# A recurrent attention, a mixture of experts and a feed-forward pair in one kernel: another way out of PSUM for the outputs, another order for the copies of the decays, whole third transposes, and a new price for strided copies

## The chip, the cores and the metric

The kernel runs on one core of a Trainium2 chip. The metric is the device time of one execution in microseconds, lower is better. The core has TensorE (PE, matrix products; PEld is its weight load), VectorE (DVE), ScalarE (ACT), GpSimd (POOL) and SyncE (SP, which here issues DMAs). Each engine works through its own queue in order.

## The reference

Three stages follow one another, all in float32.

```
# 1: 4 batches x 8 heads = 32 states of 40x40, 768 steps
y[t]  = r[t] . state
Sa    = state . a[t]
state = state * w[t] - outer(Sa, b[t]) + outer(v[t], k[t])
# 2: x = y as 3072 tokens x 320; 8 experts, the best one for each token
h = relu(x_e @ w1[e]);  out = gate * (h @ w2[e])        # 320 -> 1024 -> 320
# 3: h = out @ w_in;  g = max(h,0) + alpha*min(h,0);  result = g @ w_out   # 320 -> 2048 -> 320
```

## The kernel before

**Tiling.** The 768 steps are cut into 12 chunks of 64 steps (c = 0 to 11), taken in pairs kk = c//2. A chunk is turned into small matrix products: with the running products of the decays w, the inputs k, b and a are scaled, their products are formed, a triangular system of 64 steps per state is solved, and then the state is carried from chunk to chunk. The 32 states go in four groups of eight (z or b = 0 to 3).

**The stages of a pair.** `pro` (line 629) loads w for 128 steps, 32 steps to each quarter of the 128 partitions, as `raw` [128, 32 steps, 40]. It copies them twice into step-innermost order: `W[:,:,1:33]` and `R[:,:,1:32]` are [128, 40, 33] tiles whose last index is the step. Scans along the step then make the running products, forward in W and backward in R. Between the first scans and the multiplication that joins the two halves of a chunk stand two copies of one column of W each (`cr`, line 642). `a_load` and `kb_load` turn the products back with VectorE transposes (`turned`) and multiply the inputs by them (`prod`, lines 680 to 683). `s1a` and `s1` form the products, `solve` (line 763) does the triangular solution in 62 instructions, `g_out` and `g_load` bring the solution to the layouts that the next products read: for the first two chunks by engine copies (lines 775 to 787), for later ones through DRAM, with one copy into another order (line 747). `wg` finishes the inverse. `chain` (line 820) carries the state for one chunk and one group; its last lines 876 to 886 transpose the outputs of two groups into a PSUM tile `p` [128 tokens, 4, 104], load the decays `Px` for these tokens from DRAM and multiply: two VectorE instructions, one for each half of the heads, read `p` and `Px` and write the token tile `x`. There are 24 such blocks, so 48 instructions. The state's own decay inside `chain` (line 868) is a multiplication that may go to GpSimd or VectorE (`pv`).

**After the attention.** `route` (line 980) transposes the 320 columns of x in three pieces of 128, 128 and 64, multiplies them by the gate's weights `wg` [128, 3, 32], finds the expert and scatters the rows to `xs` in DRAM. It is called 8 times for 24 blocks of 128 tokens. `block` runs one expert, or one group of tokens of the last stage, over float32r products: `xT` (line 1141) transposes the rows in the same three pieces and splits them into a high and a low part; there are 16 such calls (9 for the experts, 7 for the last stage). Of the third piece the high part stands twice, in partitions 0 to 63 and 64 to 127, since the third weight block holds its high and low part there. `split_w` and `conv` prepare the weights, on VectorE, ScalarE and GpSimd. `pick` belongs to a branch that is not taken here.

**The order of the work.** Nothing is issued in the order in which it is written. `Sched.add` records each operation with the engines that it may go to: `copy` allows ScalarE or VectorE, `copy3` also GpSimd, `pv` GpSimd or VectorE. `Sched.cost` (line 191) gives each a price in ns, `forward` (line 344) is a list scheduler over these prices and `backward` sets due times from the result; of seven passes the one that ends first by the prices is kept, and it fixes the engine and the place of every operation, DMAs on SP's queue among them. A choice of VectorE is charged 300 ns more (`BIAS`). A matrix product whose shape class differs from the one before it on TensorE is charged 150 ns (`SWC`). The price of a copy on ScalarE between SBUF tiles is 0.8333 ns for an element and 93 ns, on VectorE 0.52 ns for an element and 69 ns, whatever the strides. One bfloat16 product of zeros after another fills idle time of TensorE in the attention (`fillers`).

## Time and profile before

| what | value |
|---|---|
| median of 3 runs | 1160.78 us (1160.41 to 1169.69) |
| the profiled execution | 1159.91 us, its span 1158.1 us |
| TensorE busy | 999.1 us, 86% of the span |
| VectorE busy | 826.7 us, 71% |
| ScalarE busy | 471.4 us, 41% |
| GpSimd busy | 255.1 us, 22% |
| mean granted TensorE clock | 0.915 |

The span runs from the first to the last instruction of the profiled execution; what lies around it is 1.8 us. The views used are the busy time by stretch of the span, the chain of work that ended last (followed back from the last instruction), the lists of instructions of one engine in order of time, the groups of equal instructions with their mean duration, and the waits by engine. In the lists a bracket behind a row is the idle time of the engine just before it and what ended it. All operations are issued through one line of the planner (L559, or L557 for the blocks of small products), so they are told apart by their tiles and shapes. Names of tiles are those of the large buffers: "w" and "f" are weight slots that the attention uses first, "plain" is the rest of SBUF, "bank" is PSUM.

### The profile page before, as it was taken

What the parts mean: (1) busy time and instruction counts of PE and PEld (TensorE: products, weight loads), DVE (VectorE), ACT (ScalarE), POOL (GpSimd) and SP (SyncE); (2) the same over time, 40 slices, a digit from 0 to 9 for tenths busy, and PEclk for the clock granted to TensorE, in tenths of its full rate; (3) what the DMA queues carried; (4) which work ended last, traced back from release to release, by engine and by line L of the source; (5) the groups of instructions that cost most, each with busy time, mean ns of one, the idle gap of its engine ahead of it and who ended that gap; (6) DMA issues with size and microseconds to landing.
All of it is one profiled execution on the core that took longest, in us unless ns stands there. A gap on an engine that the chain in (4) does not pass through costs nothing.

```text
span 1158.1 us, 31886 instructions
## 1 busy us (share of the span) xinstructions
PE 999.1 (86%) x13085; PEld 854.0 (74%) x13113; DVE 826.7 (71%) x1749; ACT 471.4 (41%) x1013; POOL 255.1 (22%) x399
## 2 busy tenths in 40 slices
PE   5743977888878888787998999999999999999995
PEld 2522865665656757576997988889999999999994
DVE  7997589779888978368876878985555555555561
ACT  7724855355364435246544444442222212121231
POOL 8401302012214222013222122341010101010241
PEclk9755797889898999869999999999999999999998
DMA  9872556576676667547665665650110000000000
GB/s 182 143 204 67 76 108 123 98 145 113 123 144 135 114 136 218 106 141 216 176 207 158 198 191 145 205 174 16 54 38 7 30 6 27 9 12 12 12 6 32
DMA packets 267476, 124.73 MB, mean 108 GB/s; under 512 B 209088, under 2 KB 254960, under 8 KB 267129
## 3 DMA queue, kind: packets, MB, share of 16 engines
q1 hardware_dynamic: 263481, 110.75, 41.6%
q0 software_dynamic: 3840, 11.85, 3.0%
q8 instruction: 105, 1.72, 0.6%
q14 instruction: 50, 0.41, 0.1%
HBM read 86.32 MB, written 41.22 MB: 110 GB/s over the span
## 4 chain that ended last, share of the span: by engine, by line
PE 33%; DMA 12%; DVE 8%; issue 3%; ACT 1%; SPq 1%; POOL 0%; POOLq 0%; DVEq 0%; ACTq 0%
PE bank L559 31%; DVE plain L559 5%; DMA plain<-in_moe_w_dram 4%; DMA ys<-plain 3%; DVE w L559 2%; DMA plain<-in_moe_w_out_dram 2%; PE bank L557 2%; DMA plain<-in_moe_w_in_dram 1%; DVE f L559 1%; DMA out_dram<-plain 1%; SPq L559 1%; DMA wout<-plain 1%; ACT w L559 1%; ACT f L559 1%; DMA plain<-ys 0%
## 5 line engine op out<-in xcount | busy, mean ns | idle before, releaser
L559 PE MATMUL bank<-f,w 128*128 128x512 f32 (+2 forms) x1472 | 329.2, 362 | 0.1
L559 PE MATMUL bank<-w,f 128*128 128x320 f32 (+1 forms) x1824 | 310.2, 313 | 10.9 <-ACT f L559 10.3
L559 PEld LDWEIGHTS bank<-w,f 128*128 128x128 f32 (+1 forms) x1824 | 282.9, 188 | 24.4 <-ACT f L559 12.3
L559 PEld LDWEIGHTS bank<-f,w 128*128 128x128 f32 x1472 | 252.4, 190 | 30.9 <-DVE f L559 0.3
L559 DVE TENSOR_SCALAR plain<-bank,plain 128x512 f32<-128x512 f32 (+2 forms) x114 | 76.4, 672 | 128.7 <-PE bank L559 128.7
L559 ACT CAST f<-plain 128x512 fp32r<-128x512 f32 (+1 forms) x96 | 56.2, 586 | 236.0 <-PE bank L559 228.9
L559 DVE TENSOR_TENSOR w<-w 128x255 f32<-128x255 f32 (+14 forms) x377 | 136.5, 362 | 12.0 <-DMA w<-LTd 5.0
L559 ACT COPY w<-bank 104x512 f32<-104x512 f32 (+9 forms) x241 | 102.6, 445 | 80.0 <-PE bank L557 51.8
L559 DVE TENSOR_TENSOR plain<-bank,w 128x256 f32<-128x256 f32 (+2 forms) x228 | 81.7, 376 | 39.3 <-PE bank L557 32.8
L559 ACT CAST w<-plain 64x256 fp32r<-64x256 f32 (+4 forms) x107 | 58.7, 561 | 88.5 <-DMA plain<-in_moe_w_dram 49.0
L557 PE MATMUL bank<-plain,w 64*64 64x104 f32 (+2 forms) x2416 | 86.7, 283 | 4.8 <-issue 2.0
L557 PE MATMUL bank<-ident,w 128*104 128x128 f32 x384 | 66.2, 311 | 25.8 <-ACT plain L559 6.7
L557 PEld LDWEIGHTS bank<-plain,w 64*64 64x64 f32 (+2 forms) x2416 | 72.6, 151 | 19.1 <-issue 9.2
L559 DVE TENSOR_TENSOR w<-plain,w 64x256 fp32r<-64x256 f32 (+3 forms) x95 | 59.5, 632 | 33.2 <-ACT w L559 31.9
L557 PE MATMUL bank<-w,w 32*32 32x32 f32 (+2 forms) x2608 | 52.8, 222 | 33.4 <-ACT w L559 27.3
L559 POOL TENSOR_TENSOR plain<-plain,w 104x160 f32<-104x160 f32 (+3 forms) x56 | 39.3, 709 | 188.6 <-DVE plain L559 159.2
L557 PEld LDWEIGHTS bank<-w,w 32*32 32x32 f32 (+2 forms) x2608 | 43.5, 132 | 46.2 <-ACT w L559 31.4
L557 PEld LDWEIGHTS bank<-ident,w 128*104 128x104 f32 x384 | 45.8, 145 | 37.8 <-ACT plain L559 7.9
L559 DVE SCALAR_TENSOR_TENSOR plain<-bank,plain 128x512 f32<-128x512 f32 (+1 forms) x112 | 68.4, 612 | 4.5
L559 ACT COPY w<-w 32x256 f32<-32x256 f32 (+7 forms) x59 | 55.3, 939 | 39.9 <-DVE w L559 34.8
L559 ACT COPY plain<-bank 128x208 f32<-128x208 f32 (+5 forms) x139 | 49.1, 393 | 53.9 <-PE bank L557 43.0
L559 PE MATMUL bank<-w 128*128 128x512 bf16 x155 | 56.6, 457 | 15.3 <-ACT w L559 10.4
(110 smaller groups left out, 1336.5 us busy)
## 6 DMA issues: line engine op xcount, KB each, us to landing
plain<-in_moe_w_dram SPq DMA_DIRECT2D x32, 320.0 KB
plain<-in_moe_w_dram SPq DMA_DIRECT2D x64, 128.0 KB
LTd<-w SPq DMA_DIRECT2D x80, 64.0 KB
plain<-in_moe_w_out_dram SPq DMA_DIRECT2D x8, 640.0 KB
wout<-plain SPq DMA_DIRECT2D x8, 640.0 KB
w<-wout SPq DMA_DIRECT2D x8, 640.0 KB
xs<-w SPq DMA_DIRECT2D x8, 608.8 KB
plain<-xs SPq DMA_DIRECT2D x7, 603.8 KB
```

The source lines that it names most:

```text
L557: for _,m,a,k in a[0]: getattr(nc.tensor,m)(*[f(x) for x in a],**{q:f(x) for q,x in k.items()})
L559: getattr(getattr(nc,e),m)(*[f(x) for x in a],**{q:f(x) for q,x in k.items()})
```

## The change

The pair of output multiplications in `chain` becomes one ScalarE copy of all 320 columns from PSUM to the token tile, and one multiplication of that tile by `Px` on SBUF, on GpSimd or VectorE as the planner chooses. The two copies of `pro` keep source and target, but run through the source in the order in which it lies and write with a stride of 33 elements, where before they read with a stride of 40 elements and wrote 32 or 31 elements in a row. In `route`, `xT` and `pick` the third transpose takes columns 192 to 319, a whole 128, in place of 256 to 319; the columns wanted then stand in partitions 64 to 127, the gate's last 64 weight rows are loaded there (the rows above them are zero), and the copies in `xT` read `p[64:128]`. In the price list a copy on ScalarE between SBUF tiles with an innermost stride (of source or target) above one element and more than 8 elements costs 1.95 ns for an element and 50 ns, and VectorE's copies and `tensor_scalar` with such an operand cost 1.0417 ns for an element and 68 ns. The settings of the planner are the same.

```diff
--- before.py
+++ after.py
@@ -238,13 +238,15 @@
         if m=='tensor_reduce':
             n=1
             for d in ops[1].shape[1:]: n*=d
+        far=any(abs(x.ap[-1][0])>1 and x.ap[-1][1]>8 for x in ops if len(x.ap)>1)
+        if e=='scalar' and far and not ps and m=='copy': return n*1.95+50
         if e=='scalar': return n*0.8333+(51 if ps else 93)+(190 if k.get('accum_out') is not None else 0)+(95 if isinstance(k.get('scale'),(VP,SV,bass.AP)) else 0)
         if e=='vector':
             if m=='reciprocal': return 6.3*n+68
             if m=='tensor_tensor_scan': return 2.1*n+70
             if m=='memset': return 1.04*n+8
             if m=='transpose': return 2.0*n+20
-            if m in('tensor_copy','tensor_scalar') and not ps and out.dtype in (F32,F32R,I32): return 0.52*n+69
+            if m in('tensor_copy','tensor_scalar') and not ps and not far and out.dtype in (F32,F32R,I32): return 0.52*n+69
             return 1.0417*n+68+(64 if m=='tensor_scalar' and ps else 0)
         if e=='gpsimd':
             if m=='memset': return 0.85*n+20
@@ -635,7 +637,7 @@
 
         t=raw.rearrange("p t e -> p e t")
         nc.gpsimd.memset(W[:,:,0],0.0); nc.gpsimd.memset(R[:,:,0:33:32],0.0)
-        s.S.copy(W[:,:,1:33],t); s.S.copy(R[:,:,1:32],t[:,:,1:32])
+        s.S.copy(W[:,:,1:33].rearrange('p e t -> p t e'),raw); s.S.copy(R[:,:,1:32].rearrange('p e t -> p t e'),raw[:,1:32])
         back=lambda y: bass.AP(y.tensor,y.offset+y.shape[1]-1,[list(y.ap[0]),[-1,y.shape[1]]])
         for i in range(0,1320,330):
             y=x[0][:,i:i+330]; nc.vector.tensor_tensor_scan(y,y,s.Z[:,0:330],0.0,op0=ALU.mult,op1=ALU.add)
@@ -883,7 +885,7 @@
             else:
                 for h in range(2): nc.sync.dma_start(out=Px[64*h:64*h+64],in_=s.prow(g,o+c%2,16*h+8*(z//2),8,1))
             xv=s.x[:,b,0:320].rearrange("p (a h e) -> p a h e",a=4,h=2); Pv=Px.rearrange("p (a h) e -> p a h e",h=2)
-            for h in range(2): nc.vector.tensor_tensor(xv[:,:,h],p[:,:,64*h:64*h+E],Pv[:,:,h],op=ALU.mult)
+            nc.scalar.copy(xv,s.two(p)); s.S.pv('tensor_tensor',xv,xv,Pv,op=ALU.mult)
         if kk==5 and c%2: s.emit_x(kk,s.x,2+z//2,1)
         elif z==3: s.emit_x(kk,s.x,0,4 if kk<5 else 2)
     def run(s):
@@ -943,7 +945,7 @@
         nc=s.nc; g=nc.gpsimd; s.S.cur='mc'
         g.memset(s.wg,0.0)
         nc.sync.dma_start(out=s.wg[:,0:2,0:NE],in_=s.w_gate[0:256,:].rearrange("(k p) e -> p k e",p=128))
-        nc.sync.dma_start(out=s.wg[0:64,2,0:NE],in_=s.w_gate[256:320,:])
+        nc.sync.dma_start(out=s.wg[64:128,2,0:NE],in_=s.w_gate[256:320,:])
         nc.sync.dma_start(out=s.al,in_=s.alpha.rearrange("(k p) -> p k",p=128))
         g.tensor_scalar(s.nal,s.al,-1.0,None,op0=ALU.mult)
         for e in range(NE):
@@ -988,11 +990,11 @@
 
         lg=s.S.psum([32*n,128],'u')
         for k in range(3):
-            w=128 if k<2 else 64; o=n*(k%(4//n)); xt=s.xt[:,o:o+n]
+            c=(0,128,192)[k]; o=n*(k%(4//n)); xt=s.xt[:,o:o+n]
             p=s.S.psum([128,n,128])
-            for j,b in enumerate(bs): nc.tensor.transpose(p[0:w,j,:],x[:,b,k*128:k*128+w],s.ident)
-            s.S.copy(xt[0:w],p[0:w])
-            for j in range(n): nc.tensor.matmul(lg[32*j:32*j+32],s.wg[0:w,k,:],xt[0:w,j,:],start=k==0,stop=k==2)
+            for j,b in enumerate(bs): nc.tensor.transpose(p[:,j,:],x[:,b,c:c+128],s.ident)
+            s.S.copy(xt,p)
+            for j in range(n): nc.tensor.matmul(lg[32*j:32*j+32],s.wg[:,k,:],xt[:,j,:],start=k==0,stop=k==2)
         lT=lT[0:32*n]
         s.S.copy(lT,lg)
         p=s.S.psum([128,n,32])
@@ -1143,12 +1145,14 @@
         nc=s.nc; r=xr.shape[0]; n=r*nt
         xh,xl=[x[:,:,0:n] for x in s.X()]; R=lambda a:a.bitcast(F32R)
         for k in range(3):
-            p=s.S.psum([128,n]); m=128 if k<2 else 64
+            p=s.S.psum([128,n]); c=(0,128,192)[k]
             for t in range(nt):
-                nc.tensor.transpose(p[0:m,t*r:(t+1)*r],xr[:,t,k*128:k*128+m],s.ident[0:r,0:r])
-            s.S.copy(R(xh[0:m,k,:]),p[0:m])
-            if k==2: s.S.copy(R(xh[64:128,k,:]),p[0:64])
-            nc.vector.tensor_tensor(R(xl[0:m,k,:]),p[0:m],xh[0:m,k,:],op=ALU.subtract)
+                nc.tensor.transpose(p[:,t*r:(t+1)*r],xr[:,t,c:c+128],s.ident[0:r,0:r])
+            if k<2:
+                s.S.copy(R(xh[:,k,:]),p); nc.vector.tensor_tensor(R(xl[:,k,:]),p,xh[:,k,:],op=ALU.subtract)
+            else:
+                for h in (0,64): s.S.copy(R(xh[h:h+64,k,:]),p[64:128])
+                nc.vector.tensor_tensor(R(xl[0:64,k,:]),p[64:128],xh[64:128,k,:],op=ALU.subtract)
         return xh,xl,n,r
     def gemm1(s,w,X):
 
@@ -1275,13 +1279,10 @@
     nc=s.nc; st=S_[:,0:8]; sc=S_[:,8:16]; l=S_[:,32:40]; ex=S_[:,40:48]; oh=S_[:,48:52].bitcast(BF16)
     p=s.S.psum([128,3,128])
     for k in range(3):
-        n=128 if k<2 else 64
-        nc.tensor.transpose(p[0:n,k,:],x[:,k*128:k*128+n],s.ident)
-    s.S.copy(xt[:,0:2,:],p[:,0:2,:]); s.S.copy(xt[0:64,2,:],p[0:64,2,:])
+        c=(0,128,192)[k]; nc.tensor.transpose(p[:,k,:],x[:,c:c+128],s.ident)
+    s.S.copy(xt,p)
     lg=s.S.psum([128,NE])
-    for k in range(3):
-        n=128 if k<2 else 64
-        nc.tensor.matmul(lg,xt[0:n,k,:],s.wg[0:n,k,0:NE],start=k==0,stop=k==2)
+    for k in range(3): nc.tensor.matmul(lg,xt[:,k,:],s.wg[:,k,0:NE],start=k==0,stop=k==2)
     nc.vector.tensor_copy(l,lg)
     nc.vector.tensor_reduce(st[:,0:1],l,axis=AX.X,op=ALU.max)
     nc.vector.scalar_tensor_tensor(sc,l,st[:,0:1],s.rev,op0=ALU.is_equal,op1=ALU.mult)
```

## Rows read from the trace of the kernel before

**Rows 1.** The page, chain that ended last: share of the span by engine.
```profile
PE 33%; DMA 12%; DVE 8%; issue 3%; ACT 1%; SPq 1%; POOL 0%; POOLq 0%; DVEq 0%; ACTq 0%
```
**Rows 2.** Busy us by stretch: length, PE, PEld, DVE, ACT, POOL (instructions), clock, DMA share, GB/s.
```profile
0.00:102.00 102.00, 52.91 (x488) 31.59 (x493) 88.53 (x129) 50.89 (x102) 40.33 (x100) 0.71 0.82 161
102.00:150.00 48.00, 39.70 (x1007) 33.03 (x1009) 28.64 (x71) 37.51 (x74) 15.01 (x49) 0.71 0.48 77
150.00:475.00 325.00, 268.82 (x7157) 206.80 (x7176) 269.87 (x760) 158.72 (x390) 65.62 (x107) 0.90 0.65 132
475.00:781.00 306.00, 274.96 (x2264) 247.65 (x2264) 235.15 (x462) 137.22 (x280) 78.44 (x79) 0.94 0.60 176
```
**Rows 3.** The chain in order of time: start us, us, what.
```profile
781.08 342.25 PE bank L559 x2024
```
**Rows 4.** VectorE in order of time: start us, us, operation, count, [idle before <- releaser].
```profile
15.00 1.53 DVE L559 TENSOR_TENSOR w<-w 128x1320 f32<-128x1320 f32 x1 [3.03 <-POOL w L559]
...
115.88 0.42 DVE L559 COPY w<-bank 128x256 f32<-128x256 f32 x1 [5.03 <-PE bank L557]
```
**Rows 5.** ScalarE in order of time, in the same columns.
```profile
9.21 2.68 ACT L559 COPY f<-f 128x1280 f32<-128x1280 f32 x1
...
14.38 0.53 ACT L559 COPY w<-w 32x40 f32<-32x40 f32 x2
...
111.62 4.29 ACT L559 COPY w<-w 32x512 f32<-32x512 f32 x4
```
**Rows 6.** TensorE in order of time: the first product after the first solution.
```profile
102.30 0.31 PE L557 MATMUL bank<-w,w 32*32 32x32 f32 x2 [20.91 <-ACT w L559]
```
**Rows 7.** TensorE's waits, 150 to 475 us: total us, times, longest.
```profile
PE bank L557 <- ACT w L559: 9.9, 11, 2.0
...
PE bank L557 <- POOL plain L559: 3.9, 3, 3.2
```
**Rows 8.** Copies and transposes by form: count, busy us, mean ns, idle before.
```profile
L559 ACT COPY w<-w 128x1280 f32<-128x1280 f32 x2 | 5.4, 2691 | 3.6 <-DMA w<-in_w_dram 3.6
L559 ACT COPY w<-w 64x1280 f32<-64x1280 f32 x6 | 7.5, 1257 | 0.7 <-DVE w L559 0.6
L559 DVE COPY w<-w 128x1280 f32<-128x1280 f32 x3 | 4.2, 1404 | 6.9 <-DMA w<-in_w_dram 6.9
L559 ACT COPY w<-w 32x1024 f32<-32x1024 f32 x6 | 12.1, 2010 | 1.3 <-DVE w L559 1.3
L559 DVE STREAM_TRANSPOSE w<-w 64x1280 f32<-64x1280 f32 x10 | 26.6, 2659 | 0.1
```
**Rows 9.** VectorE in order of time: a transpose of contiguous tiles.
```profile
100.33 1.25 DVE L559 STREAM_TRANSPOSE w<-w 128x1024 f32<-128x1024 f32 x1
```
**Rows 10.** By form: the output multiplications, and rows near the new operations.
```profile
L559 DVE TENSOR_TENSOR plain<-bank,w 128x160 f32<-128x160 f32 x48 | 14.2, 316 | 4.8 <-PE bank L557 2.4 <-DMA w<-PX 2.0 <-DMA xs<-plain 0.3
L559 ACT COPY plain<-bank 128x320 f32<-128x320 f32 x24 | 9.0, 435 | 6.6 <-PE bank L559 6.6
L559 POOL TENSOR_TENSOR plain<-plain,w 128x320 f32<-128x320 f32 x10 | 8.2, 849 | 16.4 <-DMA plain<-in_b_dram 8.0 <-DMA w<-LTd 6.3 <-ACT w L559 2.2
L559 DVE TENSOR_TENSOR w<-w,w 128x320 f32<-128x320 f32 x8 | 4.2, 529 | 1.0 <-DMA w<-in_b_dram 0.6 <-DVE w L559 0.4
```
**Rows 11.** TensorE in order of time in its unbroken stretch: whole and half-wide transposes.
```profile
836.42 0.60 PE L559 MATMUL bank<-ident,plain 128*128 128x128 f32 x4
836.77 0.82 PE L559 MATMUL bank<-w,f 128*128 128x320 f32 x4
...
837.67 0.60 PE L559 MATMUL bank<-ident,plain 128*64 128x128 f32 x4
838.02 1.13 PE L559 MATMUL bank<-w,f 128*128 128x320 f32 x6
```
**Rows 12.** ScalarE in order of time: the longest wait of its queue for a load.
```profile
492.39 1.05 ACT L559 CAST w<-plain 128x512 fp32r<-128x512 f32 x2 [9.64 <-DMA plain<-in_moe_w_dram]
```
**Rows 13.** TensorE in order of time: the wait behind it.
```profile
493.97 0.49 PE L557 MATMUL bank<-plain 40*64 40x64 f32 x8 [6.98 <-ACT plain L559]
```

## The prediction

> **What bounds the kernel now.** I read the chain of work that ended last first. It is made of TensorE for a third of the span, with DMA, VectorE and issue behind it [rows 1], and the shares do not add up to the span, because the chain cannot be followed back to the start. Its longest piece is one unbroken run of 2024 products from 781 to 1123 us [rows 3]: there only TensorE's own work counts. What happens earlier reaches the end only as far as it moves the start of that run. So the second view is the busy time by stretch [rows 2]. From 0 to 102 us VectorE is busy for 88.5 us and TensorE for 52.9, so the startup is VectorE's. From 102 to 150 us ScalarE is the busiest of the three helpers, 37.5 of 48 us, and VectorE is idle for 48 - 28.6 = 19.4 us. From 150 to 475 us TensorE (268.8 of 325) and VectorE (269.9) are both at 83%, and neither is full: the queues wait for each other in turn. From 475 to 781 us TensorE is at 275.0 of 306.
>
> The third view is the list of each engine in order of time. At 15.00 us VectorE has been idle for 3.03 us [rows 4]. The row names GpSimd as releaser, but the instruction joins the halves of a chunk and reads the `cr` columns, and these are two ScalarE copies of 0.53 us together that start at 14.38 us, behind strided copies of `pro` that ran from 9.21 us on, the first 2.68 us long [rows 5]. So 3 us of the startup are a ScalarE queue that the planner priced too low: its price for 1280 elements is 0.8333 x 1280 + 93 = 1160 ns, and the rows show 2691 [rows 8]. At 102.30 us TensorE starts after an idle 20.91 us, released by ScalarE [rows 6]. ScalarE then carries the strided copies of `g_load`: four of 512 elements take 4.29 us at 111.62 us [rows 5], about 1.07 us each where the planner counted 520 ns, and beside them VectorE is idle for 5.03 us [rows 4].
>
> **The change part by part.** The sum is made against the profiled execution, 1159.91 us, whose span is 1158.1; the median of the runs is 0.87 us above it.
>
> **New prices in the startup.** Of the prices, what counts is where the planner now puts the strided copies. On ScalarE they are charged 1.95 x 1280 + 50 = 2546 ns, on VectorE 1.0417 x 1280 + 68 = 1401 plus the bias of 300, and both figures stand near the rows (2691 and 1404 [rows 8]). It then sees the queue that holds `cr` back. The bound on one side is the whole idle time, -3.0 us. On the other side the two copies of the second `pro` go to VectorE, which is the startup's bound, and cost 2 x 1.4 = 2.8 us there: that cancels the gain, -0.2. VectorE is idle only while it waits for `cr`, so a planner that puts `cr` first gets most of it: I take -2.5.
>
> **New prices at 102 to 150 us.** Eight copies of 512 elements and sixteen of 256 (lines 779 to 787, both chunks) are planned here. At VectorE's strided rate (1404 / 1280 = 1.10 ns an element [rows 8]) one of 512 elements takes about 0.56 us. Half of the eight moved shorten ScalarE's line by 4 x 1.07 = 4.3 us, and the smaller ones by as much again. More than TensorE's idle time in this stretch, 48 - 39.7 = 8.3 us [rows 2], can't be won, and nothing is won if the products wait for something else (slow products at a granted clock of 0.71, loads). Bounds 0 to -8.3; I take -3.5, somewhat under the middle, since part of TensorE's busy time here is filler that would grow with any wait.
>
> **The copies of `pro` in reading order.** No row shows ScalarE writing with a stride. The bounds are the contiguous price, 1257 ns, and the price of the strided read, 2691 [rows 8]. The nearest row is a strided write on VectorE: the transposes of `turned`, which write with a stride, take 2659 ns for 1280 elements [rows 8], and a contiguous one 1.25 us for 1024 [rows 9], which would be 1.56 for 1280. So there a strided write costs 70% more, and I take no saving. At the other bound each copy that stays on ScalarE is 1.43 us shorter; in the startup this lies inside the 3.0 us already counted, later ScalarE is half idle (158.7 of 325 us) and hides it.
>
> **The outputs, and the balance from 150 to 475 us.** Removed: 48 x 0.316 = 15.2 us of VectorE [rows 10] by the mean (the row's busy time is 14.2, overlaps left out). Added: 24 ScalarE copies of 320 columns at 0.435 = 10.4 us, and 24 multiplications, 0.849 us on GpSimd or 0.529 on VectorE. I take two thirds on GpSimd, since VectorE pays the bias and is the busier: 16 x 0.849 = 13.6 us of GpSimd, 8 x 0.529 = 4.2 of VectorE. The new prices also push the six copies of 1024 elements that ScalarE now does (2010 ns [rows 8]) towards VectorE, at 1.10 ns an element 6 x 1.13 = 6.8 us there and 12.1 less on ScalarE. VectorE: -15.2 + 4.2 + 6.8 = -4.2 us, 1.6% of its 269.9. ScalarE: +10.4 - 12.1 = -1.7. If VectorE were the bound throughout, -4.2 would come out; if neither engine were, 0. The two share the place with TensorE, so I take -1.0. GpSimd goes up by 13.6 on 65.6 us, a fifth, and TensorE waited 3.9 us for it [rows 7], for the state's decays of line 868, which stand in the same queue as the new multiplications: a fifth of 3.9 is +0.8, between 0 and one whole instruction in front of some of the 44 decays (case 4 below).
>
> **The last outputs.** Here two VectorE instructions, 0.63 us, become a copy and a multiplication, 0.435 + 0.849 = 1.28 at most, before the last tokens can be routed. That is +0.65 us on that path; the first expert's blocks are the cover, and TensorE is at 275 of 306 us there, so it is not full. I take +0.5.
>
> **The whole transposes.** Four whole transposes start at 836.42 us and the next product 0.35 us later; four half-wide ones start at 837.67 and the next product again 0.35 us later [rows 11]. Same price, and the copies behind them keep their count and size. I take 0, bounds -0.3 and +0.3 (16 calls by 0.02 us, the reading error). What hides the rest of the step is nothing: in this stretch TensorE has no idle time, so a difference would be seen.
>
> The Trainium skill, in TensorEngine Tiling (Array Packing), section Key Properties, says that a change of the tiling mode drains TensorE, which would speak for a gain here; with the planner's own charge of 150 ns for a change of shape, twice for each of 16 + 8 calls, the sum would be 7.2 us lower. The trace doesn't agree: 0.35 us stands beside 0.35 [rows 11].
>
> Sum: -2.5 - 3.5 + 0 - 1.0 + 0.8 + 0.5 + 0 = -5.7 us. 1159.91 - 5.7 = 1154.2; with the 0.87 of the median 1155. I give 1154.0, the profiled figure.
>
> **The rivals.**
> Case 2, a larger gain. At 493.97 us TensorE has been idle for 6.98 us [rows 13], because ScalarE's queue stood for 9.64 us at a cast whose weights had not landed [rows 12], with the state's copies behind it. This is an accident of the order, and all orders change with the prices. If it goes, and the bounds of the parts above come out: 1160.8 - 3.0 - 8.3 - 4.2 - 7.0 = 1138. For it: ScalarE's errors of price, the cause of late casts, become smaller. Against: the accident isn't in what the change touches, and late weights stay late. I place it at 1138 to 1149.
> Case 3, no gain: the strided copies of the startup go to VectorE and take back what `cr` wins, and the copies at 102 us were not what the products waited for: 1160.8 - 0.2 + 0.8 = 1161. For it: VectorE is at 88.5 of 102 us. Against: idle 3.03 us just there.
> Case 4, slower. The new multiplication waits for a load (`Px`, through SP's queue of DMAs) at the head of GpSimd's queue, or the new ScalarE copy waits there for the transposes, and the state's decays and copies stand behind it, as at 493.97 us. Each such stall costs TensorE up to 6.98 us [rows 13]; the case decides from two of them on: 1160.8 + 2 x 7.0 = 1175. For it: 24 new instructions in each of two in-order queues, where the two-instruction form kept the wait on VectorE. Against: TensorE's waits for GpSimd sum to only 3.9 us in 325 [rows 7].
> Case 5, the drain: if a change of shape did cost 150 ns, 1154.0 - 7.2 = 1147. The equal steps of 0.35 us speak against it [rows 11]. The rule cited above from the Trainium skill, TensorEngine Tiling (Array Packing), section Key Properties, is of this kind.
>
> **How the numbers follow.** Case 1, the sum with its smaller errors, 1147 to 1160: 36 in 100. Case 2: 29. Case 3: 15. Case 4: 18. Case 5: 2. A difference of over 1%, 11.6 us, is about what a measurement of this kernel can tell from no change: below 1149.2 faster, above 1172.4 slower. Faster: case 2, case 5 and 5 of case 1, 0.36. Slower: 16 of the 18 of case 4. The rest, 0.48, is within 1%. The likeliest case is the first, so 1154.0, and its own range is 1147 to 1160. The range for 8 in 10 takes in case 2 to its bound and the nearer half of case 4: 1137 to 1174.
>
> **What the profile after would show.** Right: VectorE's idle time before the 1320-column multiplication near 15 us falls under 1 us; the copies of 512 elements near 112 us are spread over ScalarE, VectorE and GpSimd, and TensorE's first product of the carried state comes some 5 us earlier; 24 ScalarE copies of 128x320 and about 16 GpSimd multiplications of that shape replace the 48 of 128x160; ScalarE's strided copies of 1280 elements still take 2.6 us; transposes of 128 columns keep 0.35 us for four. The unbroken run of TensorE then starts some 6 us before 781 us with the same length. Wrong: copies of 1280 elements on ScalarE near 1.3 us would overthrow the step on reading order; a long bracket before a GpSimd or ScalarE row from 150 to 475 us, with TensorE waiting behind it, is case 4; a run after 781 us that is longer or shorter would overthrow the zero for the transposes.

## The result and the profile after

The changed kernel takes 1149.43 us (median; 1146.70 to 1152.16), the kernel before 1161.70, measured beside it. The ratio is 0.9887, 95% interval [0.9843, 0.9932]: 1.1% faster, just over the 1% that such a measurement can tell from no change. In a second measurement (run e5 below) it was 0.9897 [0.9869, 0.9924]. The forecast was 1154.0 us, 0.6% faster. The profiled execution took 1151.04 us with a span of 1149.2, which is 8.9 us less than before.

Busy time by stretch of the kernel after, in the columns of [rows 2] (length, PE, PEld, DVE, ACT, POOL with instructions, clock, DMA share, GB/s):

```profile
0.00:102.00 102.00, 65.48 (x768) 37.32 (x768) 88.36 (x130) 59.33 (x122) 54.31 (x132) 0.84 0.85 168
102.00:150.00 48.00, 39.81 (x1173) 32.68 (x1177) 41.80 (x101) 28.35 (x71) 12.26 (x18) 0.80 0.52 91
150.00:475.00 325.00, 259.45 (x6676) 201.57 (x6668) 265.48 (x704) 149.74 (x381) 72.74 (x119) 0.84 0.64 130
475.00:781.00 306.00, 286.14 (x2392) 256.84 (x2391) 238.47 (x457) 143.72 (x296) 89.05 (x87) 0.95 0.60 175
```

The reader is to see three things. From 102 to 150 us ScalarE fell from 37.5 to 28.4 us of work and VectorE rose from 28.6 to 41.8: the strided copies of 512 elements changed engine, which is 4.1 us of VectorE's rise (7 x 0.592, rows below), and work of the next pair moved here besides. From 150 to 475 us no engine's busy time moved by more than 3% of the stretch. And from 475 to 781 us TensorE was idle for 306 - 286.1 = 19.9 us, where it had been idle for 306 - 275.0 = 31.0 [rows 2]. TensorE's mean granted clock also differs: 0.84 and 0.80 in the first two stretches (0.71 and 0.71 before) and 0.84 from 150 to 475 us (0.90 before); no run here separates what that is worth.

The long run in the chain of the kernel after (start us, us, what), which answers [rows 3]:

```profile
768.61 343.81 PE bank L561 x2033
```

It starts 12.5 us earlier than before and is 1.6 us longer. The way there starts on VectorE (kernel after, VectorE in order of time, columns as in [rows 4]; the row of 62 is the triangular solution, the row at 115.88 a copy of `g_load`):

```profile
11.69 1.51 DVE L561 TENSOR_TENSOR w<-w 128x1320 f32<-128x1320 f32 x1
...
18.12 1.30 DVE L561 COPY f<-f 128x1280 f32<-128x1280 f32 x1
23.27 2.67 DVE L561 STREAM_TRANSPOSE w<-w 64x1280 f32<-64x1280 f32 x1 [3.85 <-POOL w L561]
25.80 2.39 DVE L561 COPY w<-f 128x1240 f32<-128x1240 f32 x1
...
67.43 23.43 DVE L561 TENSOR_TENSOR w<-w 128x31 f32<-128x31 f32 x62
92.06 3.76 DVE L561 TENSOR_TENSOR_SCAN w<-w 128x330 f32<-128x330 f32 x4
97.61 5.17 DVE L561 TENSOR_TENSOR_SCAN w<-w 128x330 f32<-128x330 f32 x4
...
115.88 0.59 DVE L561 COPY w<-w 32x512 f32<-32x512 f32 x1
```

The same places in the kernel before, rows that were not shown above:

```profile
60.45 4.52 DVE L559 TENSOR_TENSOR_SCAN w<-w 128x330 f32<-128x330 f32 x6
66.31 1.57 DVE L559 TENSOR_TENSOR_SCAN w<-w 128x330 f32<-128x330 f32 x2
...
76.81 23.48 DVE L559 TENSOR_TENSOR w<-w 128x31 f32<-128x31 f32 x62
```

The multiplication of 1320 columns starts at 11.69 us with no idle time ahead, where it had waited 3.03 us until 15.00 [rows 4]. Eight scans of the next pair stood ahead of the first solution and now stand behind it, so the solution starts 9.4 us earlier and ends at 90.9 us in place of 100.3. TensorE's first product of the carried state (64x64 tiles) starts at 120.22 us; before it started at 127.86.

The costs of the operations that the change touches, by form (count, busy us, mean ns, idle before), which answer [rows 8, 10]:

```profile
L561 ACT COPY plain<-bank 128x320 f32<-128x320 f32 x48 | 19.4, 435 | 19.4 <-DMA xs<-plain 9.1 <-PE bank L561 6.6 <-PE bank L559 3.4
L561 POOL TENSOR_TENSOR plain<-plain,w 128x320 f32<-128x320 f32 x15 | 13.5, 915 | 28.4 <-ACT w L561 12.6 <-ACT plain L561 9.6 <-PE bank L559 6.3
L561 DVE TENSOR_TENSOR plain<-plain,w 128x320 f32<-128x320 f32 x21 | 11.0, 525 | 15.8 <-ACT plain L561 7.4 <-POOL plain L561 3.4 <-DMA w<-PX 2.9
L561 DVE COPY w<-w 32x1024 f32<-32x1024 f32 x9 | 9.6, 1066 | 0.2
L561 ACT COPY w<-w 128x1240 f32<-128x1240 f32 x3 | 7.3, 2441 | 5.2 <-DMA w<-in_w_dram 5.2
L561 ACT COPY w<-w 128x1280 f32<-128x1280 f32 x2 | 5.1, 2526 | 0.0
L561 DVE COPY w<-w 128x1240 f32<-128x1240 f32 x2 | 4.8, 2388 | 0.0
L561 DVE COPY w<-w 128x1280 f32<-128x1280 f32 x3 | 4.4, 1477 | 7.6 <-DMA w<-in_w_dram 7.6
L561 DVE COPY w<-w 32x512 f32<-32x512 f32 x7 | 4.1, 592 | 0.2
```

ScalarE's copies of 320 columns out of PSUM went from 24 to 48. GpSimd's multiplications of this form went from 10 to 15 only. Run e7 below has the order of this kernel with the old outputs and shows 9 of this form on GpSimd and 3 on VectorE, so of the 24 new ones 6 are on GpSimd and 18 on VectorE.

Last, TensorE's waits from 475 to 781 us (total us, times, longest). First the kernel before, in a stretch for which they were not shown above, then the kernel after:

```profile
PE bank L559 <- ACT f L559: 10.3, 6, 2.9
PE bank L557 <- ACT plain L559: 7.0, 1, 7.0
PE bank L559 <- DMA plain<-xs: 4.6, 1, 4.6
PE bank L559 <- DVE f L559: 3.1, 2, 2.6
PE bank L559 <- DVE plain L559: 2.0, 3, 1.1
```

```profile
PE bank L559 <- DVE plain L561: 5.1, 1, 5.1
PE bank L561 <- DMA plain<-xs: 5.0, 2, 4.5
PE bank L561 <- ACT f L561: 3.4, 7, 1.0
PE bank L561 <- DVE plain L561: 2.6, 2, 1.9
PE bank L561 <- DVE f L561: 1.7, 4, 0.8
```

The waits for ScalarE's conversions into the tiles "f" shrank from 10.3 to 3.4 us. The single wait of [rows 13] did not go: it is the 5.1 us put down to VectorE here, in place of 7.0 put down to ScalarE. VectorE's queue stood for ScalarE, and ScalarE's queue again stood at a cast whose weights had not landed, as in [rows 12] (kernel after, a row each of TensorE, VectorE and ScalarE in order of time):

```profile
489.80 0.36 PE L559 MATMUL bank<-ident,plain 104*104 104x104 f32 x2 [5.10 <-DVE plain L561]
488.46 0.69 DVE L561 TENSOR_TENSOR w<-plain,w 128x512 fp32r<-128x512 f32 x1 [5.00 <-ACT w L561]
487.81 1.00 ACT L561 CAST w<-plain 128x512 fp32r<-128x512 f32 x2 [5.86 <-DMA plain<-in_moe_w_dram]
```

**Where the 8.9 us are.** The medians differ by 12.3 us, the two profiled executions by 8.9, and only the latter can be split into stages. The start and the end of each stage can be read from the first state product, the last scatter of rows to `xs` (the end of the state stage) and the long run. Up to the first state product: 127.86 to 120.22, -7.6 us. From there to the last scatter to `xs` (536.9 before, 533.0 after): 409.0 us before, 412.8 after, +3.7. From there to the long run: 244.2 before, 235.6 after, -8.6. The run: +1.6. From its end to the end of the span (34.8 before, 36.8 after): +2.0. Together -8.9 us. So the startup won somewhat more than was forecast, the state stage gave half of it back, and the experts' stage won more than the startup, which the sum of the prediction did not have.

Of the -8.6 us between the last scatter and the long run, 6.6 are idle time of TensorE (19.3 us before, 12.7 after), and the "ACT f" waits shown above all lie there. In the state stage TensorE's idle time rose, from 70.7 to 76.3 us. From 150 to 475 us its waits for VectorE grew from 12.6 to 27.4 us in all, and those for ScalarE fell from 25.2 to 13.4. The line that grew most, before and after:

```profile
PE bank L559 <- DVE plain L559: 3.6, 6, 1.8
```

```profile
PE bank L561 <- DVE plain L561: 15.5, 8, 6.4
```

The longest of these, 6.4 us, ends at 248.77 us, and VectorE was at work all that time, among others on scans and strided copies of the next pair; the other profiles in the order of after have it too (4.8 to 7.2 us).

### The profile page after: what moved, and what is told of

It reads as the page before. It is cut to its first block, busy times and chain, and to the rows that moved or that the text cites. A ratio compares the mean times of both kernels' runs of the same rounds, so it can differ in the third digit from the quotient of the medians.

```text
span 1149.2 us, 31868 instructions
## 1 busy us (share of the span) xinstructions
PE 1002.8 (87%) x13102; PEld 853.4 (74%) x13102; DVE 836.5 (73%) x1715; ACT 465.1 (40%) x1030; POOL 279.4 (24%) x416
## 5 line engine op out<-in xcount | busy, mean ns | idle before, releaser
L561 DVE TENSOR_TENSOR w<-w 128x240 f32<-128x240 f32 (+14 forms) x377 | 140.3, 373 | 7.0 <-DMA w<-LTd 3.6
L561 ACT COPY w<-bank 104x512 f32<-104x512 f32 (+7 forms) x242 | 102.7, 446 | 73.3 <-PE bank L559 51.2
L561 ACT CAST w<-plain 128x512 fp32r<-128x512 f32 (+4 forms) x106 | 57.5, 556 | 81.0 <-DMA plain<-in_moe_w_dram 51.4
L561 ACT COPY plain<-bank 128x208 f32<-128x208 f32 (+4 forms) x164 | 58.9, 399 | 72.6 <-PE bank L559 51.2
L561 DVE TENSOR_TENSOR plain<-bank,w 128x256 f32<-128x256 f32 (+1 forms) x180 | 67.8, 392 | 25.2 <-PE bank L559 21.3
L561 POOL TENSOR_TENSOR plain<-plain,w 104x160 f32<-104x160 f32 (+3 forms) x65 | 45.9, 712 | 157.0 <-DVE plain L561 111.6
L561 DVE TENSOR_TENSOR w<-plain,w 128x640 fp32r<-128x640 f32 (+3 forms) x92 | 63.0, 688 | 23.6 <-ACT w L561 21.9
L561 PE MATMUL bank<-w 128*128 128x512 bf16 x172 | 61.1, 492 | 7.1 <-ACT w L561 4.4
L561 POOL DMA_INDIRECT ys<-plain x32 | 37.5, 1172 | 103.9 <-DMA ys<-plain 37.7
```

Source lines behind the costliest of these rows:

```text
L561: getattr(getattr(nc,e),m)(*[f(x) for x in a],**{q:f(x) for q,x in k.items()})
```

## The experiments

**The theories.** The first: each edit has a value of its own, these add up, and the startup's gain, which the new prices bring, reaches the end. The second: each edit makes the planner lay out all operations anew, and the time is that of the laid-out order, above all of the experts' stage; the edits as such are worth little. Beside them stand rivals on single parts: the startup's gain does not reach the end, the output edit has a price or a gain of its own, the width of the transposes counts on TensorE.

All runs in one table. The ratio is to the kernel before, measured beside it, with its 95% interval; "state" is the first product of the carried state, "xs" the last scatter of the state stage, "ys" the last scatter of the experts' stage, "run" the start and length of TensorE's long run, all in us and from the one profiled execution. "Order" says whether the planner laid the operations out anew or an order was kept. The long run of e6 and e10 takes in other products (2128 and 1947, elsewhere 2023 to 2033), so its start there can't be set beside the others.

| run | what | order | ratio | state | xs | ys | run |
|---|---|---|---|---|---|---|---|
| before | | its own | 1 | 127.86 | 536.9 | 809.8 | 781.08 + 342.25 |
| after | | new | 0.9887 [0.9843, 0.9932] | 120.22 | 533.0 | 799.4 | 768.61 + 343.81 |
| e5 | the changed kernel again | of after | 0.9897 [0.9869, 0.9924] | 119.56 | 536.6 | 802.5 | 771.66 + 343.83 |
| e1 | prices alone | new | 0.9979 [0.9945, 1.0013] | 125.13 | 533.6 | 798.0 | 769.09 + 342.43 |
| e2 | all but the prices | new | 1.0127 [1.0075, 1.0179] | 124.69 | 556.2 | 820.7 | 790.53 + 343.62 |
| e3 | after, old reading order | of after | 0.9942 [0.9916, 0.9968] | 121.54 | 538.9 | 802.9 | 772.03 + 343.82 |
| e4 | before, next pair late | new | 1.0031 [1.0000, 1.0062] | 123.77 | 542.4 | 810.6 | 781.96 + 342.14 |
| e6 | before, new outputs | of before | 1.0022 [0.9995, 1.0049] | 127.33 | 549.8 | 823.1 | 775.34 + 361.32 |
| e7 | after, old outputs | of after | 0.9847 [0.9816, 0.9878] | 120.33 | 532.9 | 801.8 | 770.92 + 343.82 |
| e8 | after, half-wide transposes | new | 0.9996 [0.9973, 1.0020] | 126.01 | 548.2 | 820.4 | 790.45 + 343.42 |
| e9 | after, half-wide transposes | of after | 0.9890 [0.9854, 0.9925] | 119.10 | 534.6 | 799.7 | 768.91 + 343.88 |
| e10 | after, bias 310 | new | 1.0029 [1.0003, 1.0056] | 123.19 | 538.0 | 812.3 | 802.05 + 330.38 |
| e11 | before, bias 310 | new | 1.0017 [0.9981, 1.0052] | 124.65 | 546.7 | 823.9 | 793.97 + 343.45 |
| e12 | whole transposes alone | new | 0.9922 [0.9887, 0.9957] | 125.77 | 532.5 | 799.4 | 770.49 + 342.39 |

Two warnings on this table. Executions of one kernel spread by about 1% to either side (the kernel before took 1151.19 to 1173.76 us in 29 runs on one chip), so a single profiled execution is not a median: e1's profiled execution took 1147.77 us, its median is 1160.60. And the chips differ: the kernel before took 1161.61, 1167.70 and 1161.75 us on the three of these runs. So ratios on one chip are compared, and a stage of one profile is believed only where several profiles of the same order agree.

**e1, the prices alone.**

```diff
+        far=any(abs(x.ap[-1][0])>1 and x.ap[-1][1]>8 for x in ops if len(x.ap)>1)
+        if e=='scalar' and far and not ps and m=='copy': return n*1.95+50
...
-            if m in('tensor_copy','tensor_scalar') and not ps and out.dtype in (F32,F32R,I32): return 0.52*n+69
+            if m in('tensor_copy','tensor_scalar') and not ps and not far and out.dtype in (F32,F32R,I32): return 0.52*n+69
```

> The kernel before with the new prices alone; outputs, copies of the decays and transposes as before. Theory A (the gain is the planner's order: with true prices of strided copies it puts the second pair's decays behind the first solution, which then starts near 67 us in place of 76.8): 1150 to 1154 us, solution started by 69 us. Rival B (the gain is VectorE's relief by the output path): 1159 to 1163 us.

Measured: 1160.60 against 1161.61 us, ratio 0.9979 [0.9945, 1.0013]. The first state product came 2.7 us earlier, the solution started at 70.91 us. Theory A missed both of its numbers, and the time is rival B's, though e6 below speaks against B's reason. The prices alone don't make the gain.

**e2, everything but the prices**: the changed kernel without the lines above.

```diff
-        far=any(abs(x.ap[-1][0])>1 and x.ap[-1][1]>8 for x in ops if len(x.ap)>1)
-        if e=='scalar' and far and not ps and m=='copy': return n*1.95+50
...
-            if m in('tensor_copy','tensor_scalar') and not ps and not far and out.dtype in (F32,F32R,I32): return 0.52*n+69
+            if m in('tensor_copy','tensor_scalar') and not ps and out.dtype in (F32,F32R,I32): return 0.52*n+69
```

> The changed kernel with the old prices: outputs through ScalarE, copies of the decays in reading order and whole transposes stay. Theory A: the gain is gone, 1158 to 1163 us, the first solution again starts near 76 us. Rival B: most of the gain stays, 1148 to 1153 us.

Measured: 1175.41 us, ratio 1.0127 [1.0075, 1.0179]; both expectations missed, and the solution started at 69.56 us, not near 76. It lost in the state stage: from 124.69 to 556.2 us it took 431.5 us, where the kernel before took 409.0. The three other edits without the prices are 1.3% slower than before, the prices alone are worth 0.2%, and all four together are 1.1% faster. These don't add up, which speaks against the first theory.

**e3, the old reading order in the new order of work.** The order on every engine is that of the changed kernel; only the 12 copies of `pro` run through their source as before.

```diff
-        s.S.copy(W[:,:,1:33].rearrange('p e t -> p t e'),raw); s.S.copy(R[:,:,1:32].rearrange('p e t -> p t e'),raw[:,1:32])
+        s.S.copy(W[:,:,1:33],t); s.S.copy(R[:,:,1:32],t[:,:,1:32])
```

> The changed kernel with the decays' copies reading with a stride and writing in a row, as before. The prices of both forms are equal, so the planner's order is the same on every engine, and only these 12 instructions differ. Theory: a strided write costs ScalarE nearly what a strided read costs (2.45 us for 1240 elements in the profile after, 2.61 before), so the time differs by under 1.5 us from the changed kernel. Rival (reading in order is what made the startup shorter): 3 us or more slower than the changed kernel.

Measured: 1155.18 us, ratio 0.9942 [0.9916, 0.9968]. The copies in this kernel (by form):

```profile
L561 ACT COPY w<-w 128x1280 f32<-128x1280 f32 x2 | 5.4, 2690 | 0.0
L561 DVE COPY w<-w 128x1240 f32<-128x1240 f32 x2 | 2.7, 1364 | 0.0
```

So the strided read costs ScalarE 2690 ns where the strided write costs 2526, 6% less; and on VectorE the copy of 1240 elements costs 1364 ns when it reads with a stride and 2388 when it writes with one. What the faster copy won at 26 us was lost behind it. VectorE in order of time, e3 first and then the changed kernel of run e5:

```profile
30.92 3.71 DVE L561 TENSOR_TENSOR_SCAN f<-f,w 128x330 f32<-128x330 f32 x2
```

```profile
31.79 1.57 DVE L561 TENSOR_TENSOR_SCAN f<-f,w 128x330 f32<-128x330 f32 x2
```

In e3 these two scans began while GpSimd multiplied (three multiplications of 320 columns from 31.04 us, 2.16 us together), and took 2.1 us more. The solution then started at 69.28 us, 1.8 us later than in e5 (67.53), and the first state product 2.0 us later. The whole difference to the changed kernel, 0.9942 against 0.9897, is about 0.45%; the two intervals come from different chips and just overlap, so the reading order is worth between nothing and some 10 us here, with 2 of them seen in the startup of its one profile. By the ratios, 5 us, this is nearer to the rival's 3 us or more than to the theory's 1.5.

**e4, the startup's gain alone.** The kernel before, with the preparation of the next pair held back behind the first solution, as the changed kernel happens to have it.

```diff
-        M.consts(); M.zeros(); A.run(); M.run(); S.after('zero',CFG.get('za','ch1.3')); ...
+        M.consts(); M.zeros(); A.run(); M.run(); S.after('pro2','sol0'); S.after('zero',CFG.get('za','ch1.3')); ...
```

> The kernel before, old prices, with one edge more in the planner: the decays of the second pair may not start before the first operation of the first solution. Theory A (this place is the startup's gain): the solution starts by 69 us, the first state products come 5 to 8 us earlier than at 127.9 us, and the end 4 to 8 us earlier, 1153 to 1157 us. Rival C (the startup's gain does not reach the end, which moved for other reasons): solution early, but 1159 to 1163 us.

Measured: 1164.29 us, ratio 1.0031 [1.0000, 1.0062]. The solution began at 62.35 us and the first state product came 4.1 us earlier than before, at 123.77 us, but the state stage ended 5.5 us later, and the time is about rival C's. TensorE in order of time shows a wait late in the state stage that the kernel before does not have, small products that wait for what `g_load` brings from DRAM:

```profile
475.95 1.08 PE L557 MATMUL bank<-w,w 32*32 32x32 f32 x64 [3.06 <-DMA w<-GTd]
```

A startup that is some 4 us shorter does not by itself reach the end in this order. That part of the first theory falls.

**e5, the changed kernel again**, with no edit, to have it beside the next three on one chip.

> The changed kernel once more, beside the next three on one chip: 1147 to 1153 us if its first four runs were typical; up to 1157 if the scatter that the kernel before shows (1151 to 1174 us in 29 runs) holds here too.

Measured: 1155.41 against 1167.70 us, ratio 0.9897 [0.9869, 0.9924]. The gain repeats, on a chip that is 0.5% slower for both.

**e6, the new outputs in the order of before.** Every operation keeps its place; where the two multiplications stood, the copy and the multiplication stand. The edit puts the multiplications of three blocks in four on GpSimd (18 of 24 by the profile), a little more than the two thirds of the prediction.

```diff
             for h in range(2): nc.vector.tensor_tensor(xv[:,:,h],p[:,:,64*h:64*h+E],Pv[:,:,h],op=ALU.mult)
+            u,w=s.S.ops[-2:]; u.swap=('scalar','copy',(xv,s.two(p)),{}); w.swap=('vector' if b%3==2 else 'gpsimd','tensor_tensor',(xv,xv,Pv),{'op':ALU.mult})
```

> The kernel before with its order kept instruction by instruction, but the two VectorE multiplications of each output block carried out as one ScalarE copy and one multiplication, two blocks in three on GpSimd. It tells the worth of the new output path without a new plan. Theory A (the gain is the order of the whole plan, the path itself little): 1157 to 1164 us. Rival B (relief of VectorE by 11 us is the gain): 1150 to 1156 us.

Measured: 1170.17 us, ratio 1.0022 [0.9995, 1.0049]. The output edit, with nearly the split that the prediction assumed, changes the time by -0.05% to +0.5%.

**e7, the old outputs in the new order.** The reverse: in the order of after the two VectorE multiplications stand in the two places. The first of them stands ahead of the load of `Px` there, so half of the outputs are scaled by older decays, and for that half the wait for the load is left out.

```diff
             nc.scalar.copy(xv,s.two(p)); s.S.pv('tensor_tensor',xv,xv,Pv,op=ALU.mult)
+            for h,u in enumerate(s.S.ops[-2:]): u.swap=('vector','tensor_tensor',(xv[:,:,h],p[:,:,64*h:64*h+E],Pv[:,:,h]),{'op':ALU.mult})
```

> The changed kernel with its order kept, but each output block carried out by two VectorE multiplications out of PSUM at the two places in the order. Theory A: within 4 us of the changed kernel. Rival B: 5 to 11 us slower than the changed kernel, with VectorE 5 us or more busier from 150 to 540 us.

Measured: 1150.40 us, ratio 0.9847 [0.9816, 0.9878], beside 0.9897 of the changed kernel on the same chip. With the old outputs the order of after is as fast as with the new ones, or half a per cent faster. Since half of its waits for the load are left out, it may be faster than an exact version would be. With e6 it still says that the gain is not from the outputs' way out of PSUM; it stays when that way is undone, provided the order stays.

**e8, half-wide transposes, laid out anew**: the changed kernel with `route` and `xT` as before.

```diff
-                nc.tensor.transpose(p[:,t*r:(t+1)*r],xr[:,t,c:c+128],s.ident[0:r,0:r])
+                nc.tensor.transpose(p[0:m,t*r:(t+1)*r],xr[:,t,k*128:k*128+m],s.ident[0:r,0:r])
```

> The changed kernel with third transposes of 64 columns as before, newly planned. Theory (the width itself is worth nothing on TensorE): the unbroken run of TensorE is as long as in the changed kernel, 343.8 us within 0.6, and a difference of the whole comes from the plan alone, 1147 to 1165 us. Rival (a change of shape drains TensorE): the run is 1 us or more longer.

Measured: 1168.33 us, ratio 0.9996 [0.9973, 1.0020]. The gain is gone, and yet the long run is 343.42 us long, as with whole transposes (343.81). What changed is the order: the first state product is at 126.01 us, the state stage ends at 548.2 us (533.0 and 536.6 in the two profiles of the changed kernel), and between there and the long run TensorE waits 7.1 us for ScalarE's conversions into "f" (3.4 and 3.0).

**e9, half-wide transposes in the order of after.** Each of the 16 calls of `xT` makes the same transposes at the same place, but the third ones of 64 columns (56 in all); the copies behind them read the lower half of the bank. Nothing else differs from the changed kernel.

```diff
                 nc.tensor.transpose(p[:,t*r:(t+1)*r],xr[:,t,c:c+128],s.ident[0:r,0:r])
+                if k==2 and q is not None: q[-1].swap=('tensor','transpose',(p[0:64,t*r:(t+1)*r],xr[:,t,256:320],s.ident[0:r,0:r]),{})
```

> The changed kernel with its order on every engine, but with the second transpose of each state's last columns made of the last 64 columns alone, as before; nothing else differs. Theory (the order that the planner laid out decides, the width costs nothing): as the changed kernel, ratio to the kernel before 0.985 to 0.993, unbroken run of TensorE within 0.5 us of 343.8 us. Rival (whole transposes spare TensorE a change of tile, and e8 was slow for that): as e8, ratio near 1.000, with a run some microseconds longer or a state stage that ends later.

Measured: 1148.74 against 1161.75 us, ratio 0.9890 [0.9854, 0.9925]: the whole gain, without the whole transposes of `xT`; those of `route` stay whole in this run. Four transposes of 128 and four of 64 columns side by side in this kernel (TensorE in order of time), and its long run in the chain:

```profile
825.88 0.60 PE L562 MATMUL bank<-ident,plain 128*128 128x128 f32 x4
826.24 0.83 PE L562 MATMUL bank<-w,f 128*128 128x320 f32 x4
827.14 0.60 PE L562 MATMUL bank<-ident,plain 128*64 128x128 f32 x4
827.50 1.12 PE L562 MATMUL bank<-w,f 128*128 128x320 f32 x6
```

```profile
768.91 343.88 PE bank L562 x2033
```

From the first transpose to the next product it is 0.36 us in both cases, and the run differs by 0.07 us from the changed kernel's. The width of the transposes in `xT` costs and saves nothing on TensorE. For those of `route` no run keeps the order; in the kernel before, four whole and four half-wide ones stand ahead of equal products:

```profile
476.40 0.66 PE L559 MATMUL bank<-ident,plain 128*128 128x128 f32 x4
476.99 1.30 PE L557 MATMUL bank<-plain,w 64*64 64x104 f32 x48
...
478.58 0.63 PE L559 MATMUL bank<-ident,plain 128*64 128x128 f32 x4
479.13 1.30 PE L557 MATMUL bank<-plain,w 64*64 64x104 f32 x48
```

It is 0.59 us to the next product with whole ones and 0.55 with half-wide ones, so whole transposes save nothing there either, and what is left for e8's loss is its order.

**e10 and e11, a planner's constant that the change does not touch**: `BIAS`, the charge on a choice of VectorE, 310 in place of 300, in the changed kernel (e10) and in the kernel before (e11). Places and engines are both chosen anew.

```diff
-Sched.BIAS=300.0
+Sched.BIAS=310.0
```

> The changed kernel, with one constant of the planner that has nothing to do with the change (the bias by which it ranks operations) set from 300 to 310, so that it lays the same work out anew. Theory (the gain is that of one laid-out order): another order, another time; it may lie anywhere from 0.985 to 1.010 of the kernel before, and the gain of 1.1% is not kept as a rule. Rival (the gain belongs to the edits, whatever the order): ratio 0.985 to 0.993 again, first state product near 120 us and unbroken run starting near 770 us.

> The kernel before with the same constant set from 300 to 310. Theory (laid-out orders scatter by about as much as the change moved the time): the ratio leaves the band 0.997 to 1.003, on either side, by up to 1.5%. Rival (orders of one set of operations cost the same): within 0.3% of the kernel before, and its stall of about 7 us at 494 us is there again.

Measured: e10 1164.44 us, ratio 1.0029 [1.0003, 1.0056]; e11 1167.05 us, ratio 1.0017 [0.9981, 1.0052]. With all four edits in place and another constant the gain is gone. The startup of e10 is still good (first state product at 123.19 us, the multiplication of 1320 columns at 11.66 us with no wait), but the experts' stage is not. TensorE in order of time, e10:

```profile
491.49 0.65 PE L561 MATMUL bank<-w,plain 128*32 128x128 f32 x8 [7.37 <-ACT w L561]
...
605.13 3.56 PE L561 MATMUL bank<-w,f 128*120 128x320 f32 x12 [3.15 <-ACT f L561]
655.92 3.97 PE L561 MATMUL bank<-w,f 128*120 128x320 f32 x12 [2.86 <-ACT f L561]
```

The wait of [rows 13], 5.10 us in the changed kernel, is 7.37 us long here, and the waits for ScalarE's conversions into "f" are back, 9.7 us between the last scatter and the long run. For e11 the theory's number (outside 0.997 to 1.003) was missed: the kernel before did not get slower or faster by more than its interval, though its order changed and it shows a wait of 7.37 us at 502 us too. There the rival was right.

**e12, the whole transposes alone**, laid out anew: the kernel before with the edits in `route`, `xT` and the load of the gate's weights.

```diff
-                nc.tensor.transpose(p[0:m,t*r:(t+1)*r],xr[:,t,k*128:k*128+m],s.ident[0:r,0:r])
+                nc.tensor.transpose(p[:,t*r:(t+1)*r],xr[:,t,c:c+128],s.ident[0:r,0:r])
```

> The kernel before with the whole transposes alone, laid out anew. The edit itself costs TensorE nothing by e8. Theory (order decides): the ratio lies anywhere from 0.985 to 1.015, by where the state stage ends and the unbroken run starts (780 us before). Rival (each part has a value of its own that adds up): the four parts together gave -1.1%, e8 without this part gave 0.0%, so this part alone should give about -1.1%, ratio 0.985 to 0.993.

Measured: 1152.78 us, ratio 0.9922 [0.9887, 0.9957]. An edit that gains nothing on TensorE by e9 and the rows of `route` makes the kernel 0.8% faster when the planner lays it out anew. Busy time by stretch (columns as above), e10 first and e12 below it:

```profile
475.00:781.00 306.00, 273.49 (x2243) 244.15 (x2236) 223.40 (x439) 136.00 (x279) 75.21 (x79) 0.93 0.58 169
```

```profile
475.00:781.00 306.00, 286.89 (x2457) 257.55 (x2458) 243.12 (x474) 143.29 (x297) 83.64 (x85) 0.95 0.60 177
```

e12 has the kernel before's startup but for 2.1 us (first state product at 125.77 us) and yet the whole gain of the experts' stage: TensorE idle for 19.1 us of 306, as in the changed kernel (19.9). e10 has most of the changed kernel's startup and an experts' stage like before (32.5 us idle; before 31.0). In this pair the time goes with the experts' stage, not with the startup. It is not the only place where an order wins or loses: in e2, e4, e8 and e11 the state stage ends 5 to 19 us later than in the kernel before (table). Both theories of e12 gave ranges that hold 0.9922; what tells them apart is e9, in which the part of the same edit that lies in `xT` is worth nothing at a fixed order, and e10 and e2, which contain it and are not faster.

No version beat both kernels: e9 equals the changed one, and e7, the fastest, leaves out a wait.

## Why the prediction was right, and where its steps failed

The time came out 4.6 us below the forecast, inside the range and inside the likeliest case's own range (1147 to 1160), by the changed kernel's time in its own measurement. But the number is better than the reasons: the state stage gave back half of the startup's gain, and the experts' stage, for which the sum had no term, brought a gain of its own. That these came out so near the forecast is luck. Step by step:

**The startup: right.** The `cr` wait was to give 2.5 us of its 3.03; the multiplication starts 3.3 us earlier with no idle time. The second `pro`'s copies went to VectorE, as one bound of this step had it, and a new wait of 3.85 us stands at 23.27 us. What the prediction did not see is that the eight scans of the next pair go behind the solution: the solution gains 9.4 us, of which 6.1 are these scans (4.52 and 1.57 us in the rows above).

**The copies at 102 to 150 us: the mechanism was right, its place and worth not.** Seven of the eight copies of 512 elements went to VectorE at 592 ns (forecast: half of them, 0.56 us, some to GpSimd), and ScalarE lost 9.2 us of work. But from the end of the solution to the first state product it took 29.4 us where it had taken 27.6, because the scans now stand there (92.06 and 97.61 us). The term of -3.5 measured +1.8. The two terms together were to give -6.0 and gave -7.6.

**The copies of `pro` in reading order: nearly right.** No saving was taken for ScalarE; it is 6%, 2526 ns against 2690. The prediction's sign, copies still at 2.6 us, held (2.53). It had not thought of VectorE, where one of the two copies became 1.0 us slower and the other stayed as it was. At the whole kernel e3 leaves 0 to some 10 us open in favour of the change.

**The outputs: the split was wrong, the verdict right.** Two thirds of the multiplications were to be on GpSimd; it was 6 of 24; the planner chose VectorE for the others in spite of its bias (the rows show 525 ns there and 915 on GpSimd). VectorE's work from 150 to 475 us fell by 4.4 us (forecast 4.2), made up otherwise than thought; ScalarE's fell by 9.0 where 1.7 was forecast. The three terms, -1.0 + 0.8 + 0.5, came to +0.3 us, that is nothing. e6 gives 1.0022 [0.9995, 1.0049], and e7, which leaves out half of the waits for the load, does not show the old outputs to be slower: the edit is worth nothing or costs up to 0.5%. The 3.9 us that the term of +0.8 was taken from are one line of three [rows 7]; all of TensorE's waits for GpSimd from 150 to 475 us are 5.6 us in five waits before, the longest 3.2, and 7.7 in nine after, the longest 2.3. Case 4, a stall of TensorE behind the new instructions that costs up to 7 us, did not show in them.

**The whole transposes: right, and shown for `xT`.** 0.35 us for four was read from [rows 11]; e9 has 0.36 for four of either width in one trace, and runs of 343.88 and 343.81 us. Case 5, that a change of tile drains TensorE, falls by the same numbers. The prediction weighed the Trainium skill, TensorEngine Tiling (Array Packing), section Key Properties, on this; no run here shows its drain between 128x128 and 128x64 transposes.

**The step that failed** is the silent one, that what the startup wins reaches the end and that the experts' stage stays as it is. The sum put all of its -5.7 us ahead of 540 us and nothing behind. Measured, of -8.9 us the time up to the end of the state stage holds -3.9, and the way from there to the long run -8.6. The sum had no term for the second. The nearest thing in the prediction is case 2 (29 in 100), a gain by an accident of the order, but its accident is not what went: the wait of [rows 13] lies ahead of the last scatter, and it is still 5.10 us in the profile after and 4.3 to 6.6 us in the other four with its order (e3, e5, e7, e9), each time behind a ScalarE cast whose weights had not landed. What went, between the last scatter and the long run, are TensorE's waits for ScalarE's conversions into "f": 10.3 us before and 8.2 in e6, which has its order; 1.6 to 3.4 us in the five profiles with the order of after. The time from the last scatter to `xs` to the last one to `ys` agrees: 264.0 to 268.9 us in these five, 272.9 and 273.3 in before and e6. The other orders show that this stage alone doesn't make the time: e12 has 266.9 us and gains, e8, e10 and e11 have 272.2 to 277.2 and don't, but e1, e2 and e4 have 264.4, 264.5 and 268.2 and don't gain either (e2 and e4 end their state stage later, and e1's one profiled execution is 12.8 us shorter than its median). And e4 shows the first half of the silent step wrong: 4.1 us won at the first state product, nothing at the end. In the changed kernel too the state stage gave 3.7 of the startup's 7.6 us back.

**What stays open.** That the order decides is shown by pairs: e8 and e9 do the same work but for the transposes of `route`, in two orders, 0.9996 and 0.9890; e10 and the changed kernel differ in a constant, 1.0029 and 0.9887. The prices act through the order and the engines that the planner chooses alone; each of the other edits was undone or added by itself at a fixed order, `route` excepted. No run undid all of them at once. Why the planner lays out a better order in the changed kernel and in e12 is not shown. The laid-out orders without whole transposes lie close together (before, e1, e4, e8, e11: 0.998 to 1.003), those with them far apart (0.989, 0.992, 1.003, 1.013), so the edit may act through the planner's charge for a change of shape, which it removes; that is argued, and four orders are too few to say that it helps as a rule.

## What to carry to other kernels

Where a list scheduler places every operation, an edit is two things, its own cost and a new order of everything, and the second can be larger: hold the order fixed to price the edit (as in e3, e6, e7, e9), and change a constant that has nothing to do with it to see how far orders scatter (as in e10, e11), before the gain is put down to the edit. A gain ahead of a stage with slack is followed to the end stage by stage, not added up. Read for each stage when it starts and ends, and expect the next stage to give back part of what the one before it won.

## What the runs showed of the hardware that was not expected

**A strided write cost VectorE 1.75 times a strided read, in one of two sizes.** In the new form the copy of 31 steps by 40 takes 2388 ns (mean of 2; in the profiles of e2, e5, e8 and e10 single ones took 2.36 to 2.45 us) and the one of 32 steps by 40 takes 1.29 to 1.42 us past the first microseconds (after, e5, e8, e10), for 3% more elements; in the kernel before the two took 1362 and 1404 ns, the second in [rows 8]. The first copy of a run, near 6 us, took 1.38 to 1.75 us in after, e5 and e10, 2.40 in e8 and 4.56 in e2, and 4.66 in e12, which reads with a stride. The Trainium skill, VectorE: DVE Perf Modes, section Mode 2×_2P, makes the use of both read ports depend on an outermost dimension that is even, or odd and equal in source and target; 32 is even, and 31 is odd with a source that lies in one piece. The rows agree with this, with a factor of 1.7 to 1.9, but no run changed the 31 alone, so it is not shown.

**ScalarE gains little by writing with a stride in place of reading with one**: 2526 against 2690 ns for 1280 elements, where the contiguous copy takes 1257 [rows 8].

**Scans of two inputs beside GpSimd.** Two scans that read two tiles took 1.57 us beside GpSimd's instructions on single columns and 3.71 beside its multiplications (e5 and e3 above). The Trainium skill, SBUF — State Buffer, section Who interferes with whom, says that a VectorE instruction with two inputs in SBUF contends with a GpSimd instruction that reads SBUF; the two rows agree, at 2.1 us for the pair.
